# A planned attention and two-layer kernel: the planner counts its loads as one line, and memory features come from the transposed queries

## Chip, cores and metric

One core of one Trainium2 chip. The metric is the device time of one execution in microseconds; lower is better. The kernel before takes 1077.71 us (median of 3 runs, 1077.41 to 1077.94).

## What is computed

Attention with a memory (4 batches, 8 heads, 576 rows, 64 columns a head), then two layers of width 512 to 2048 to 512 on the 2304 rows:

```python
scores = scale * np.matmul(q, k.transpose(0, 1, 3, 2)), causal
a = np.exp(scores - scores.max(-1, keepdims=True))
a /= a.sum(-1, keepdims=True) + 1e-09
local = np.matmul(a, v)
phi(x) = np.where(x > 0, x, np.exp(x) - 1.0) + 1.0
mem_out = einsum('bhsd,bhde->bhse', phi(q), M_prev) / (einsum('bhsd,bhd->bhs', phi(q), z_prev)[..., None] + 1e-6)
x = g * mem_out + (1 - g) * local                 # g = sigmoid(beta), one for each head
layer 1: h = x @ w_in;  x = max(0.01 h, h) @ w_out
layer 2: h = x @ w_in;  out = (h - tanh(h)) @ w_out
```

## The kernel before

The work is cut into 32 units, each of two heads of one batch. A unit of kind A has the first 256 query rows, one of kind B the other 320. Four units of a batch and kind fill an x tile of 256 rows (the last 64 rows of each batch go to a ninth tile, R). A unit loads `qk` (transposed queries and keys), `rq` (queries in rows), `zb` and `mb` (z and M of its two heads), and `v`. Its memory part: phi of `rq` (ScalarE twice, L500 and L503; VectorE's max, L506), z times phi summed for each row tile and head (L513, four or six multiply-and-sum pairs on VectorE), reciprocal and gate (L519, L523), division of phi (L530), transposes of phi on TensorE (L547), a copy out of PSUM (pT, by the helper's L399 or L401), and the product with the block-diagonal M (L670), which opens the accumulator `o`. Its score part: scores (L584, L589: arrays of 64 rows, two heads side by side), maxima with the mask (L610), exponentials with sums (L630), for each row tile of two heads the sum with epsilon and gate and its reciprocal (L637, L641), scaling (L647 to L651: ScalarE, VectorE or POOL). Last come transposes of the weights (L691, L703), their copies, and the values (L725: arrays of 64 columns), added into `o`.

Layer 1 takes an x tile, splits it into a high and a low part (`xs`, lines L399, L401, L412 of the helpers) and sweeps over eight pairs of weight columns: `up` matmuls (L851), leaky step (L930), high and low part, `dn` matmuls (L953). The first four tiles go through two pairs first (four sweeps of 48 up and 48 dn matmuls each), then through the rest. The weights are 64-bit numbers: each 128x512 piece is loaded, turned into float32 by five steps (L783 on ScalarE, L786 to L799 on VectorE), and split (L399 to L412). Layer 2 has its weights converted beside layer 1, stored, and loaded again. It is written out by hand after the plan (L1060 on) and its matmuls are L851 and L1120.

The order of everything up to layer 2 comes from `Schedule` (L86). Each piece of work has engines with a cost each, a priority, and buffers from rings of fixed size (`RINGS`, L33). `run` (L146) goes through time on its own costs: whenever an engine is free it takes the piece of best priority whose inputs are done and whose buffers are free. A load costs its issue on SyncE, and a fixed latency (2300 to 4000 ns) later its readers may start, however many loads are under way. Attention has the better priority, layer matmuls fill in. What stands in the program is only the order on each engine; on the chip each instruction waits in its engine's queue for what it needs.

Of the kernel before, what the change touches and what calls it, by code (L numbers as in the profile page):

```python
# [9 lines left out]
F32 = mybir.dt.float32  # L10
# [26 lines left out]
}  # L37

# [42 lines left out]
class Op:  # L81
    __slots__ = (
        "alts", "fn", "prio", "lat", "alloc", "deps", "users", "left", "tiles", "end", "engine", "idx", "port")


class Schedule:  # L86


    def __init__(self, rings):
        self.rings = {k: [None] * n for k, n in rings.items()}  # L90
        self.count = {k: 0 for k in rings}
        self.made = {k: 0 for k in rings}
        self.ops = []

# [50 lines left out]

    def run(self):  # L146
        engines = ("pe", "act", "dve", "pool", "sp")
        free = {e: 1000.0 for e in engines}
# [11 lines left out]
        cold = 0.0  # L160
        port_free = 0.0
        events = [1000.0]
        t = -1.0
        while todo:
# [6 lines left out]
            while again:  # L171
                again = False
                for e in engines:
                    if free[e] > t:
                        continue
                    for i, (_, _, at, o) in enumerate(ready[e]):
# [25 lines left out]
                    free[e] = mine  # L202
                    heapq.heappush(events, mine)
# [24 lines left out]
CW = 256  # L228

# [15 lines left out]
def kernel(  # L245
# [40 lines left out]

    identr = const.tile([128, 128], F32R, name="identr")
    mask = const.tile([128, 512], BF16, name="mask")
    mask4 = const.tile([128, S // 2], BF16, name="mask4")
    omg4 = const.tile([128, H // 2], F32, name="omg4")  # L290
    mbs = [const.tile([128, 128], F32, name=f"mb{i}") for i in range(RINGS["mb"])]
    gate = const.tile([128, H], F32, name="gate")
# [22 lines left out]
    for m in mbs:  # L315
        nc.gpsimd.memset(m, 0.0)
# [3 lines left out]
    nc.sync.dma_start(out=gate, in_=beta.partition_broadcast(128))  # L320
    nc.scalar.activation(out=gate, in_=gate, func=AF.Exp, scale=-1.0)
    nc.vector.tensor_scalar(out=gate, in0=gate, scalar1=1.0, scalar2=None, op0=ALU.add)
    nc.vector.reciprocal(out=gate, in_=gate)
    nc.vector.tensor_scalar(out=omg, in0=gate, scalar1=-1.0, scalar2=1.0, op0=ALU.mult, op1=ALU.add)

    nc.vector.tensor_scalar(out=omg, in0=omg, scalar1=1e-30, scalar2=None, op0=ALU.max)
    nc.vector.reciprocal(out=omg, in_=omg)
    for i in range(2):
        p = slice(64 * i, 64 * i + 64)
        nc.vector.tensor_copy(out=omg4[p], in_=omg[p].rearrange("p (h j) -> p h j", j=2)[:, :, i])  # L330

# [48 lines left out]
    att = pa.enter_context(tc.tile_pool(name="att", bufs=1, side="right"))  # L380
    s_p = pa.enter_context(tc.tile_pool(name="s", bufs=3, space=PSUM, side="right"))
# [3 lines left out]
    x_h = {}  # L385
# [31 lines left out]
    class Unit:  # L417
# [14 lines left out]
        def declare(self, pr, prev):  # L432
# [15 lines left out]
            qk, rq, zb, mb, v_ = new("qk"), new("rq"), new("zb"), new("mb"), new("v" if kind == "B" else "va")  # L448
# [9 lines left out]
            def load_q(e):  # L458
                rq.tile = att.tile([128, 3, 2, 64], F32, name="rq", bufs=RINGS["rq"])
                for i, h in enumerate(heads):  # L460
                    nc.sync.dma_start(
                        out=rq.tile[:, 0:nq, i, :],
                        in_=q[b, h, q0 * 128:(q0 + nq) * 128, :].rearrange("(t p) d -> p t d", p=128))

            def load_mz(e):
                zb.tile = att.tile([128, 2, 64], F32, name="zb", bufs=RINGS["zb"])
                nc.sync.dma_start(
                    out=zb.tile.rearrange("p h d -> p (h d)"),
                    in_=z_prev[b, 2 * hp:2 * hp + 2, :].rearrange("h d -> (h d)").partition_broadcast(128))
# [15 lines left out]

            op([("sp", 600)], load_qk, alloc=[qk], lat=3000)
            op([("sp", 1000)], load_q, alloc=[rq], lat=2300)
            op([("sp", 1500)], load_mz, alloc=[zb, mb], lat=2300)
            op([("sp", 1000)], load_v, alloc=[v_], lat=2300)
# [3 lines left out]
            ph, dn = new("ph"), new("dnm")  # L493

            def flat(t):
                return t.rearrange("p t h d -> p (t h d)")[:, 0:nf]

            def phi_neg(e):
                ph.tile = att.tile([128, 3, 2, 64], F32, name="ph", bufs=RINGS["ph"])
                nc.scalar.activation(out=flat(ph.tile), in_=flat(rq.tile), func=AF.Relu, scale=-1.0)  # L500

            def phi_exp(e):
                nc.scalar.activation(out=flat(ph.tile), in_=flat(ph.tile), func=AF.Exp, scale=-1.0)  # L503

            def phi_max(e):
                nc.vector.scalar_tensor_tensor(  # L506
                    out=flat(ph.tile), in0=flat(rq.tile), scalar=1.0, in1=flat(ph.tile), op0=ALU.add, op1=ALU.max)

            def phi_den(e):
                dn.tile = att.tile([128, 3, 2], F32, name="dn", bufs=RINGS["dnm"])  # L510
                for i in range(nq):
                    for j in range(2):
                        nc.vector.tensor_tensor_reduce(  # L513
                            out=rq.tile[:, i, j, :], in0=ph.tile[:, i, j, :], in1=zb.tile[:, j, :], scale=1.0,
                            scalar=1e-6, op0=ALU.mult, op1=ALU.add, accum_out=dn.tile[:, i, j:j + 1])

            def den_inv(e):
                d = dn.tile[:, 0:nq, :]
                nc.vector.reciprocal(out=d, in_=d)  # L519

            def den_gate(e):
                d = dn.tile[:, 0:nq, :]
                nc.vector.tensor_tensor(  # L523
                    out=d, in0=d, in1=gate[:, 2 * hp:2 * hp + 2].unsqueeze(1).to_broadcast([128, nq, 2]),
                    op=ALU.mult)

            def phi_div(e):
                p = ph.tile[:, 0:nq].rearrange("p t h d -> p (t h) d")
                d = dn.tile[:, 0:nq].rearrange("p t h -> p (t h)")
                (nc.vector if e == "dve" else nc.gpsimd).tensor_tensor(  # L530
                    out=p, in0=p, in1=d.unsqueeze(2).to_broadcast([128, 2 * nq, 64]), op=ALU.mult)
# [9 lines left out]
            s, pT = new("s"), new("pT")  # L541

            def tr_p(e, s=s):
                pT.tile = att.tile([128, 320], F32, name="pT", bufs=RINGS["pT"])
                s.tile = s_p.tile([128, 512], F32, name="s")
                for i in range(nq):
                    nc.tensor.transpose(  # L547
                        s.tile[:, i * 128:(i + 1) * 128], ph.tile[:, i].rearrange("p h d -> p (h d)"), ident)

            def p_out(e, s=s):  # L550
                copy(e, pT.tile[:, 0:nqc], s.tile[:, 0:nqc])
# [670 lines left out]
```

## Time and profile before

| | |
|---|---|
| runs | 1077.41, 1077.71, 1077.94 us |
| profiled execution | span 1076.9 us from first to last instruction; no other time of it is given |
| TensorE matmul busy | 1042.5 us, 97% |
| VectorE, ScalarE, POOL busy | 754.0, 637.7, 100.3 us |
| mean granted clock of TensorE | 0.989 |
| DMA | 102.5 MB, 116403 packets |

A busy TensorE is not an engine at its peak, since matmuls are pipelined; the distance between starts tells what one costs. Two instructions of VectorE may overlap a little in the rows, so there too the distance between starts is the cost in a full queue.

### The profile page before, as it was taken

The page shows a single profiled execution, that of the slowest core. Times are in us where ns is not written, and L with a number is a line of the kernel's source. Part 1 is how long each engine was busy: PE and PEld are TensorE (multiplying, and loading weights), DVE is VectorE, ACT ScalarE, POOL GpSimd, SP SyncE. Part 2 cuts the span into 40 slices and gives each one's busy share as a digit, 9 for nine tenths or more (in the row PEclk, how much of TensorE's full clock was granted, in tenths as well). Part 3 has the DMA queues.
Part 4 walks back from the last instruction along what each step waited for, and adds up shares of the span by engine and source line. Part 5 has one row for each costly group of instructions (what it writes and reads, how often), then busy time and mean ns, then how long its engine had stood idle before and what let it go on. Part 6 is the DMA issues. An engine that isn't in the chain of part 4 may idle for free.

```text
span 1076.9 us, 20416 instructions
## 1 busy us (share of the span) xinstructions
PE 1042.5 (97%) x7488; PEld 918.8 (85%) x7488; DVE 754.0 (70%) x2049; ACT 637.7 (59%) x1357; POOL 100.3 (9%) x102
## 2 busy tenths in 40 slices
PE   4799999999999999999999999999999999999997
PEld 2477799778689978979999999999999999999996
DVE  6999999888677587664212366867777676777765
ACT  5889876777673277361101134766666666666664
POOL 0001000000000000000000000221222222222221
PEclk9699999999999999999999999999999999999999
DMA  7867763655644354243100055010101101010000
GB/s 223 250 177 222 225 203 107 159 153 153 183 141 137 119 165 147 89 132 102 40 2 21 10 158 186 1 41 1 40 2 39 40 1 40 1 40 20 1 20 20
DMA packets 116403, 102.52 MB, mean 95 GB/s; under 512 B 63824, under 2 KB 92496, under 8 KB 116304
## 3 DMA queue, kind: packets, MB, share of 16 engines
q1 hardware_dynamic: 115088, 99.91, 31.2%
q10 hardware_dynamic: 1216, 1.31, 0.4%
q8 instruction: 59, 0.97, 0.4%
q14 instruction: 40, 0.33, 0.1%
HBM read 78.65 MB, written 22.54 MB: 94 GB/s over the span
## 4 chain that ended last, share of the span: by engine, by line
PE 83%; DMA 6%; DVE 5%; ACT 4%; issue 1%; SPq 1%; DVEq 0%; ACTq 0%
PE up L851 36%; PE dn L1120 18%; PE dn L953 18%; PE s L703 3%; PE o L725 3%; PE s L584 3%; PE s L589 1%; PE o L670 1%; DMA cv<-in_moe_w_in_dram 1%; DMA qk<-in_qkt_dram 1%; ACT e L630 1%; DMA x2s<-g 1%; DMA w<-in_moe_w_in_dram 1%; DMA vs<-cv 1%; ACT e L647 1%
## 5 line engine op out<-in xcount | busy, mean ns | idle before, releaser
L851 PE MATMUL up<-xs,w 128*128 128x256 f32 x3456 | 454.6, 284 | 0.4 <-ACT g L930 0.4
L851 PEld LDWEIGHTS up<-xs,w 128*128 128x128 f32 x3456 | 434.1, 190 | 12.4 <-issue 5.6
L953 PE MATMUL dn<-gh,w 128*128 128x256 f32 x1152 | 160.1, 286 | 0.0
L953 PEld LDWEIGHTS dn<-gh,w 128*128 128x128 f32 x1152 | 146.0, 192 | 7.2 <-issue 6.5
L1097 DVE SCALAR_TENSOR_TENSOR gf<-u,w 128x512 f32<-128x512 f32 x72 | 85.8, 1192 | 83.4 <-ACT w L1094 83.4
L1120 PE MATMUL dn<-w,gh 128*128 128x512 f32 x568 | 143.2, 394 | 0.6 <-ACT gh L1107 0.6
L412 POOL TENSOR_TENSOR gl<-gf,gh 128x512 fp32r<-128x512 f32 x71 | 92.2, 1299 | 506.9 <-ACT gh L1107 503.3
L930 ACT ACTIVATE g<-up 128x512 f32<-128x512 f32 x72 | 42.9, 595 | 146.4 <-PE up L851 138.9
L1120 PEld LDWEIGHTS dn<-w,gh 128*128 128x128 f32 x568 | 101.6, 188 | 19.8 <-ACT gh L1107 0.8
L1089 ACT ACTIVATE u<-up 128x512 f32<-128x512 f32 x72 | 43.0, 598 | 123.7 <-PE up L851 123.7
L630 ACT ACTIVATE e<-e,mx 128x128 f32<-128x128 f32 (+4 forms) x144 | 82.7, 576 | 11.0 <-DVE mx L610 4.6
L953 PE MATMUL dn<-gl,w 128*128 128x256 f32 x576 | 84.5, 285 | 0.0
L401 DVE CAST gh<-g 128x512 fp32r<-128x512 f32 x35 | 14.9, 427 | 96.9 <-ACT g L930 96.8
L953 PEld LDWEIGHTS dn<-gl,w 128*128 128x128 f32 x576 | 75.2, 192 | 2.1 <-issue 1.9
L1120 PE MATMUL dn<-w,gl 128*128 128x512 f32 x284 | 76.2, 390 | 0.0
L610 DVE CUSTOM_DVE_ANT_0 e<-s,mask 128x128 f32<-128x128 f32 (+4 forms) x144 | 63.7, 483 | 10.6 <-PE s L584 6.6
L399 ACT ACTIVATE pt<-s 128x320 f32<-128x320 f32 (+4 forms) x149 | 58.2, 435 | 17.6 <-PE s L691 9.0
L584 PE MATMUL s<-qk 64*128 64x128 f32 (+3 forms) x256 | 53.8, 497 | 14.8 <-DMA qk<-in_qkt_dram 10.4
L703 PE MATMUL s<-identr,e 128*128 128x128 f32 x448 | 64.0, 287 | 3.9 <-ACT pT L399 2.8
L1120 PEld LDWEIGHTS dn<-w,gl 128*128 128x128 f32 x284 | 53.3, 188 | 11.9
L703 PEld LDWEIGHTS s<-identr,e 128*128 128x128 f32 x448 | 51.0, 145 | 12.9 <-ACT pT L399 3.4
L1091 DVE SCALAR_TENSOR_TENSOR hu<-up,u 128x512 f32<-128x512 f32 x72 | 49.7, 690 | 16.6 <-ACT u L1089 16.5
(105 smaller groups left out, 1334.2 us busy)
## 6 DMA issues: line engine op xcount, KB each, us to landing
w<-in_moe_w_out_dram SPq DMA_DIRECT2D x16, 512.0 KB, 5.1
cv<-in_moe_w_in_dram SPq DMA_DIRECT2D x32, 256.0 KB, 2.9
vs<-cv SPq DMA_DIRECT2D x64, 128.0 KB, 1.8
cv<-in_moe_w_out_dram SPq DMA_DIRECT2D x32, 256.0 KB, 2.9
v<-vs SPq DMA_DIRECT2D x32, 256.0 KB, 3.1
w<-in_moe_w_in_dram SPq DMA_DIRECT2D x14, 512.0 KB, 5.0
qk<-in_qkt_dram SPq DMA_DIRECT2D x16, 448.0 KB, 3.7
v<-in_v_dram SPq DMA_DIRECT2D x16, 320.0 KB, 3.5
```

What stands on the lines that cost most here:

```text
L399: nc.scalar.activation(out=out, in_=in_, func=AF.Copy)
L412: (nc.vector if e == "dve" else nc.gpsimd).tensor_tensor(out=out, in0=in_, in1=high, op=ALU.subtract)
L584: nc.tensor.matmul(ss[j].tile[:, c0:c0 + nn], lhsT=qk.tile[p, a:a + 128], rhs=qk.tile[p, kc:kc + nn], start=True, stop=True)
L610: nc.vector.tensor_tensor_reduce(out=out, in0=in0, in1=in1, scale=-scale, scalar=mx.tile[:, 0:1] if t == 4 and j else BIG, op0=ALU.add, op ...
L630: nc.scalar.activation(out=x, in_=x, func=AF.Exp, scale=-1.0, bias=mx.tile[:, k:k + 1], accum_out=sm.tile[:, j:j + 1])
L703: nc.tensor.transpose(ss[j].tile[:, a:a + 128], x, ident)
L851: nc.tensor.matmul(ps()[:, s, :], lhsT=w[:, wh * 512 + kt * 128:wh * 512 + (kt + 1) * 128], rhs=xs()[:, xh, kt, :], start=(kt == 0 and j = ...
L953: nc.tensor.matmul(dn[m // 2].tile[:, m % 2, :], lhsT=w[:, wh * 512 + m * 128:wh * 512 + (m + 1) * 128], rhs=gg.tile[:, s * 256:(s + 1) * ...
L1089: nc.scalar.activation(out=u, in_=h, func=AF.Square)
L1091: nc.vector.scalar_tensor_tensor(out=hu, in0=h, scalar=c4, in1=u, op0=ALU.mult, op1=ALU.mult)
L1097: nc.vector.scalar_tensor_tensor(out=g, in0=u, scalar=lin, in1=w, op0=ALU.mult, op1=ALU.add)
L1120: nc.tensor.matmul(dn[t], lhsT=g[:, c0:c0 + 128], rhs=w[:, wh * 512:(wh + 1) * 512], start=(p == 0 and s == 0 and j == 0), stop=(p == NP - ...
```

## The change

The memory part is turned round. phi is taken from the transposed queries in `qk`, so no `rq` is loaded and no phi transposed. M and z of all eight heads of a batch are loaded at once (`mz`: four pairs, 128 x 130, block-diagonal M with z as an extra column for each head; zeroed once by POOL) for four units. One product for each row tile gives result and denominator together in a score bank (128x130). VectorE adds epsilon and multiplies by 1/g, takes the reciprocal, and multiplies the result into `mo`; TensorE transposes `mo` straight into the accumulator `o`. The sums of the exponentials stand in one tile of five columns a unit: A has one epsilon step and one reciprocal for both row tiles, B two (sm, `GROUPS`), before all scalings.

The planner gets: a line of eight load lanes with sizes (`send`), so that a load lands after those ahead of it; no weight load (`calm`) while the line is over 6 us behind; a price for changing between TensorE's array shapes (`SWITCH`); other start times and costs. The two early weight loads are the first thing on ScalarE, and the gate's steps are part of the plan.

```diff
-    "qk": 2, "rq": 2, "xr": 1, "zb": 2, "mb": 2, ..., "pT": 1, "mx": 6, "sm": 6,
+    "qk": 2, "xr": 1, "mz": 2, ..., "mo": 1, "mx": 6, "sm": 3,
+LANES = 8
+SWITCH = {(0, 1): 88.0, (2, 1): 88.0, (0, 2): 45.0}
+CALM = 6000.0
+GROUPS = {"A": ((0, 2),), "B": ((0, 1), (1, 2), (2, 3))}
...
+    def send(self, t, sizes):
+        for size in sizes:
+            k = self.sent % LANES
+            t = max(t, self.lanes[k])
+            took = size / 375.0
+            self.landed = self.lanes[k] = max(self.landed + max(180.0, took), t + 2000.0 + took)
+            self.sent += 1
+            t += 600.0
+        return t
...
-        free = {e: 1000.0 for e in engines}
+        free = {"pe": 2500.0, "act": 2200.0, "dve": 3200.0, "pool": 4000.0, "sp": 800.0}
...
+                        if o.dma:
+                            if o.calm and self.landed > t + CALM:
+                                continue
+                            mine = self.send(t, o.dma)
+                            o.lat = self.landed - mine
                         if e == "pe":
+                            if o.mode != mode:
+                                mine += SWITCH.get((mode, o.mode), 0.0)
...
+    early_raw = [wts.tile([128, 1024], I32, name=f"w0_{f}") for f in range(EARLY)]
+    for f, raw in enumerate(early_raw):
+        nc.scalar.dma_start(out=raw..., in_=w1_in[...])
...
+    mzs = [att.tile([128, H // 2, 130], F32, name=f"mz{i}") for i in range(RINGS["mz"])]
+    for m in mzs:
+        nc.gpsimd.memset(m, 0.0)
...
             def load_mz(e):
+                mz.tile = mzs[mz.seq % RINGS["mz"]]
+                for j in range(2):
+                    rows, c = slice(j * 64, (j + 1) * 64), j * 65
+                    nc.sync.dma_start(out=mz.tile[rows, :, c:c + 64], in_=m_prev[b]...[j])
+                    nc.sync.dma_start(out=mz.tile[rows, :, c + 64], in_=z_prev[b]...[j])
...
-            op([("act", ACT(nf))], phi_neg, reads=[rq], alloc=[ph])
-            op([("act", ACT(nf))], phi_exp, reads=[ph], writes=[ph])
-            op([("dve", DVE(nf))], phi_max, reads=[rq, ph], writes=[ph])
-            op([("dve", 2 * nq * 145)], phi_den, reads=[ph, zb], writes=[rq], alloc=[dn])
-            op([("dve", 110)], den_inv, reads=[dn], writes=[dn], port=False)
-            op([("dve", 75)], den_gate, reads=[dn], writes=[dn])
-            op(lows(nf), phi_div, reads=[ph, dn], writes=[ph])
-            order["p"] = op([("pe", nq * 109 + 50)], tr_p, reads=[ph], alloc=[s, pT], after=in_order("p"))
-            free_op(copies(nqc, True), p_out, reads=[s], writes=[pT], port=False)
+            op([("act", ACT(nqc))], phi_neg, reads=[qk], alloc=[ph])
+            op([("act", ACT(nqc))], phi_exp, reads=[ph], writes=[ph])
+            op([("dve", DVE(nqc))], phi_max, reads=[qk, ph], writes=[ph])
+            order["p"] = op([("pe", nq * 195)], mem, reads=[ph, mz], alloc=[s, mo], after=in_order("p"))
+            free_op([("dve", 75)], den_gate, reads=[s, gates], alloc=[dn], port=False)
+            free_op([("dve", 110)], den_inv, reads=[dn], writes=[dn], port=False)
+            free_op([("dve", DVE(nf))], mem_out, reads=[s, dn], writes=[mo], port=False)
...
-            op([("pe", nqc * 1.67)], mem, reads=[mb, pT], alloc=[o])
+            op([("pe", nq * 109 - 60)], mem_tr, mode=2, reads=[mo], alloc=[o])
```

New lines that the order below names: product L535, its gate, reciprocal and multiplication L544, L551 and L554, transposes of the result L695, phi L520 to L527, scores L597, weight transposes L729, values L751, up L878, sums' steps L659 and L664, scaling L679, conversion L809 to L825, high and low parts L424, L426 and L437.

ScalarE, its first instructions, before (`gate` is the gate of beta, `w_0` the first early weight load):

```order
L321 ACT_TABLE_LOAD
L321 ACTIVATE gate<-gate 128x8
L342 DMA w_0_182<-in_moe_w_in_dram 128x4x256
L342 DMA w_1_186<-in_moe_w_in_dram 128x4x256
L500 ACTIVATE ph<-rq 128x256
L503 ACTIVATE ph<-ph 128x256
```

and now:

```order
L318 DMA w_0_65<-in_moe_w_in_dram 128x4x256
L318 DMA w_1_66<-in_moe_w_in_dram 128x4x256
L520 ACT_TABLE_LOAD
L520 ACTIVATE ph<-qk 128x256
L524 ACTIVATE ph<-ph 128x256
L809 ACTIVATE cv<-w_0_65 128x512
```

The loads stand ahead of the table load and of the gate, which comes later.

VectorE around the low halves of the first x tile (`xs`), before; four multiply-and-sum pairs (L513) stand just ahead of this piece:

```order
L641 RECIPROCAL sm<-sm 128x2
L637 SCALAR_TENSOR_TENSOR sm<-sm,omg 128x2
L519 RECIPROCAL dn<-dn 128x4
L412 TENSOR_TENSOR xs<-x,xs 128x512
L523 TENSOR_TENSOR dn<-dn,gate 128x4
L649 TENSOR_SCALAR e_650<-e_650,sm 128x128
L401 CAST xs<-x 128x512
L530 TENSOR_TENSOR ph<-ph,dn 128x256
L412 TENSOR_TENSOR xs<-x,xs 128x512
```

and now:

```order
L437 TENSOR_TENSOR xs<-x,xs 128x512
L664 RECIPROCAL sm<-sm 128x4
L815 TENSOR_SCALAR cv<-cv 128x512
L679 TENSOR_SCALAR e_497<-e_497,sm 128x128 x2
L679 TENSOR_SCALAR e_501<-e_501,sm 128x256 x2
L437 TENSOR_TENSOR xs<-x,xs 128x512
```

The second low half stood at row 209 of VectorE's order and stands at row 131; one reciprocal serves both row tiles, and all four scalings of a unit are VectorE's here.

TensorE around the first up matmul of layer 1 (`w_0` the first weights, `mb` and `mz` the memory's matrices), before:

```order
L584 MATMUL s<-qk 128x128 x2
L584 MATMUL s<-qk 128x256 x2
L547 MATMUL s<-identr,ph 128x128 x2
L851 MATMUL up<-xs,w_0_276 128x256 x6
L670 MATMUL o<-pT,mb_69 128x256
L725 MATMUL o<-pt,va 64x256 x2
```

and now:

```order
L729 MATMUL s<-identr,e_497 128x128
L729 MATMUL s<-identr,e_501 128x128 x2
L878 MATMUL up<-xs,w_0_258 128x256 x9
L535 MATMUL s<-mz_168,ph 128x130 x2
L878 MATMUL up<-xs,w_0_258 128x256 x3
L878 MATMUL up<-xs,w_1_311 128x256 x12
L695 MATMUL o<-identr,mo 128x128 x2
L751 MATMUL o<-pt,va 64x256 x2
```

The product into a score bank comes first, layer matmuls stand between it and the transposes into `o`.

## Rows read from the trace of the kernel before

**Rows 1.** Busy time by stretch: us, engines' busy us (x count), clock, DMA share, GB/s

```profile
10.00:56.00 46.00, 32.28 (x143) 19.40 (x144) 42.11 (x200) 37.64 (x115) 0.00 (x0) 0.78 0.82 250
56.00:106.00 50.00, 48.20 (x380) 38.51 (x380) 49.58 (x257) 46.50 (x146) 3.66 (x5) 1.00 0.72 198
200.00:400.00 200.00, 196.21 (x1497) 161.24 (x1497) 146.76 (x563) 120.77 (x295) 1.53 (x10) 1.00 0.53 152
540.00:660.00 120.00, 120.00 (x1002) 120.00 (x1002) 47.48 (x85) 25.45 (x43) 0.00 (x0) 1.00 0.21 66
```

The engines stand in the order PE (TensorE matmul), PEld (its weight loads), DVE (VectorE), ACT (ScalarE), POOL.

**Rows 2.** The same view, two stretches of 5 us

```profile
25.00:30.00 5.00, 1.03 (x5) 0.28 (x2) 3.73 (x17) 4.50 (x16) 0.00 (x0) 0.64 1.10 300
55.00:60.00 5.00, 4.29 (x34) 3.06 (x31) 5.00 (x22) 3.46 (x13) 0.00 (x0) 1.00 0.92 225
```

**Rows 3.** Order of time, first 12 us: start, us, engine, line, what [idle before]

```profile
0.80 1.28 ACT L321 ACT_TABLE_LOAD   x1 [0.80 <-PEq L1207]
...
3.73 1.00 ACTq L342 DMA_DIRECT2D w<-in_moe_w_in_dram  x2
...
5.60 0.55 SPq L454 DMA_DIRECT2D qk<-in_qkt_dram  x1
...
9.33 0.66 ACT L783 ACTIVATE cv<-w 128x512 f32<-128x512 f32 x1 [3.48 <-DMA w<-in_moe_w_in_dram]
10.02 0.43 DVE L786 TENSOR_SCALAR cv<-cv 128x512 f32<-128x512 f32 x1 [3.71 <-ACT cv L783]
```

**Rows 4.** Order of time, VectorE alone, 41.6 to 44.8 us

```profile
41.49 0.28 DVE L649 TENSOR_SCALAR e<-e,sm 128x128 f32<-128x128 f32 x1
41.69 0.16 DVE L637 SCALAR_TENSOR_TENSOR sm<-sm,omg 128x2 f32<-128x2 f32 x1
41.76 0.29 DVE L610 CUSTOM_DVE_ANT_0 e<-s,mask 128x128 f32<-128x128 f32 x1
...
42.18 0.42 DVE L610 CUSTOM_DVE_ANT_0 e<-s,mask 128x256 f32<-128x256 f32 x1
...
42.95 0.41 DVE L506 SCALAR_TENSOR_TENSOR ph<-rq,ph 128x256 f32<-128x256 f32 x1
43.27 0.35 DVE L649 TENSOR_SCALAR e<-e,sm 128x256 f32<-128x256 f32 x1
43.53 0.22 DVE L513 CUSTOM_DVE_ANT_0 rq<-ph,zb 128x64 f32<-128x64 f32 x1
...
44.11 0.69 DVE L412 TENSOR_TENSOR w<-cv,w 128x512 fp32r<-128x512 f32 x1
44.71 0.17 DVE L519 RECIPROCAL dn<-dn 128x4 f32<-128x4 f32 x1
```

**Rows 5.** Order of time, TensorE alone, 76 to 106 us

```profile
76.58 0.60 PE L670 MATMUL o<-pT,mb 128*128 128x256 f32 x2
77.10 0.87 PE L725 MATMUL o<-pt,va 128*64 128x256 f32 x8
77.90 0.50 PE L953 MATMUL dn<-gl,w 128*128 128x256 f32 x2
78.24 0.82 PE L703 MATMUL s<-identr,e 128*128 128x128 f32 x6
78.81 1.43 PE L953 MATMUL dn<-gh,w 128*128 128x256 f32 x10
80.17 0.93 PE L584 MATMUL s<-qk 64*128 64x128 f32 x8
81.03 0.74 PE L953 MATMUL dn<-gh,w 128*128 128x256 f32 x4
...
105.95 1.24 PE L851 MATMUL up<-xs,w 128*128 128x256 f32 x9
```

A unit's values, scores and product stand as eight, eight and two matmuls in the trace.

**Rows 6.** The same view, 41 to 43 us

```profile
41.67 1.55 PE L725 MATMUL o<-pt,va 128*64 128x256 f32 x8
```

**Rows 7.** Waits of TensorE: who for whom, us in total, times, longest

```profile
PE s L703 <- ACT pT L399: 2.8, 1, 2.8
```

More of the change, by code (lines that the diff above doesn't have):

```diff
@@ L82 @@
     __slots__ = (
-        "alts", "fn", "prio", "lat", "alloc", "deps", "users", "left", "tiles", "end", "engine", "idx", "port")
+        "alts", "fn", "prio", "lat", "alloc", "deps", "users", "left", "tiles", "end", "engine", "idx", "port", "dma", "calm", "mode")
 class Schedule:
@@ L159, in run @@
         todo = len(self.ops)
-        cold = 0.0
+        cold, mode = 0.0, 0
         port_free = 0.0
-        events = [1000.0]
+        events = sorted(set(free.values()))
         t = -1.0
@@ L289 @@
     mask4 = const.tile([128, S // 2], BF16, name="mask4")
-    omg4 = const.tile([128, H // 2], F32, name="omg4")
-    mbs = [const.tile([128, 128], F32, name=f"mb{i}") for i in range(RINGS["mb"])]
-    gate = const.tile([128, H], F32, name="gate")
+    omg5 = const.tile([128, H // 2, 5], F32, name="omg5")
+    ginv = const.tile([128, H], F32, name="ginv")
     omg = const.tile([128, H], F32, name="omg")
@@ L319 @@
     nc.vector.memset(thr_t, -T2)
[L320 to L330, printed above, removed]
     wt = [[None] * NF for m in range(2)]
@@ L502, in phi_exp @@
             def phi_exp(e):
-                nc.scalar.activation(out=flat(ph.tile), in_=flat(ph.tile), func=AF.Exp, scale=-1.0)
+                nc.scalar.activation(out=ph.tile[:, 0:nqc], in_=ph.tile[:, 0:nqc], func=AF.Exp, scale=-1.0)
             def phi_max(e):
                 nc.vector.scalar_tensor_tensor(
[L507 to L531, printed above, removed]
@@ new lines, in den_gate, with den_inv @@
+            def den_gate(e):
+                dn.tile = att.tile([128, 3, 2], F32, name="dn", bufs=RINGS["dnm"])
+                nc.vector.scalar_tensor_tensor(
+                    out=dn.tile[:, 0:nq], in0=banked()[:, :, :, 64], scalar=1e-6,
+                    in1=ginv[:, 2 * hp:2 * hp + 2].unsqueeze(1).to_broadcast([128, nq, 2]),
+                    op0=ALU.add, op1=ALU.mult)
+            def den_inv(e):
+                d = dn.tile[:, 0:nq]
+                nc.vector.reciprocal(out=d, in_=d)
@@ L559, in declare @@
             made = {}
+            sm = new("sm")
+            sums = 2 * nq - (kind == "B")
+            first, expos, inv = [], {}, {}
             for tiles in ([[0, 1]] if kind == "A" else [[2], [3], [4]]):
@@ L727, in pv @@
                             rhs=pt.tile[:, at + j * w:at + (j + 1) * w], start=False, stop=kt == nk - 1)
[L729 removed]
+            op([("pe", 801 if kind == "A" else 2205)], pv, mode=1, reads=[v_, o] + list({id(x): x for x in pts.values()}.values()),
                writes=[o])
@@ L803, in convert @@
         if early:
-            sc.op([("act", 500)], load, alloc=[raw], lat=3600, prio=(-2, 0))
-        else:
-            op([("sp", 500)], load, alloc=[raw], lat=2600, after=after)
-        first = op([("act", ACT(n))], c_abs, reads=[raw], alloc=[g])
+            raw.tile = early_raw[f]
+            sc.op([("sp", 1)], lambda e: None, alloc=[raw], lat=3500.0 + 1400.0 * f, prio=(-2, 0))
+        else:
+            op([("sp", 500)], load, alloc=[raw], dma=[1024 * n], calm=True, after=after)
+        first = op([("act", ACT(n) + 45)], c_abs, reads=[raw], alloc=[g])
         op([("dve", DVE(n / 2))], c_max, reads=[g], writes=[g])
@@ L986, in layer1, with load_beta, gate_exp, gate_rest @@
                 sop(copies(512, True), x2_out, reads=[dn[i]], alloc=[x2], port=False)
-            sop([("sp", 500)], x2_store, reads=[x2], writes=[x2_h[n] if p1 == NP else xp_h[n][i]], lat=2300)
+            sop([("sp", 500)], x2_store, reads=[x2], writes=[x2_h[n] if p1 == NP else xp_h[n][i]], dma=[262144])
+    def load_beta(e):
+        nc.sync.dma_start(out=ginv, in_=beta.partition_broadcast(128))
+    def gate_exp(e):
+        nc.scalar.activation(out=ginv, in_=ginv, func=AF.Exp, scale=-1.0)
+    def gate_rest(e):
+        nc.vector.tensor_scalar(out=ginv, in0=ginv, scalar1=1.0, scalar2=None, op0=ALU.add)
+        nc.vector.reciprocal(out=omg, in_=ginv)
+        nc.vector.tensor_scalar(out=omg, in0=omg, scalar1=-1.0, scalar2=1.0, op0=ALU.mult, op1=ALU.add)
+        nc.vector.tensor_scalar(out=omg, in0=omg, scalar1=1e-30, scalar2=None, op0=ALU.max)
+        nc.vector.reciprocal(out=omg, in_=omg)
+        pairs = omg.rearrange("p (h j) -> p h j", j=2)
+        for i in range(2):
+            nc.vector.tensor_copy(out=omg5[:, :, 2 * i:2 * i + 2], in_=pairs)
+        for i in range(2):
+            p = slice(64 * i, 64 * i + 64)
+            nc.vector.tensor_copy(out=omg5[p, :, 4], in_=pairs[p, :, i])
+    gates = sc.new(None)
+    sc.op([("sp", 600)], load_beta, writes=[gates], prio=(0, 0.1), dma=[4096])
+    sc.op([("act", 210)], gate_exp, reads=[gates], writes=[gates], prio=(0, 0.1))
+    sc.op([("dve", 1600)], gate_rest, reads=[gates], writes=[gates], prio=(0, 0.1))
     prev = None
```

159 lines of the change are left out of this document (87 added, 72 removed), and 2 rows, old and new, of the table RINGS.

## The prediction

> **What bounds the kernel now.** I read the profile in this order. First the busy times by stretch [rows 1]: from 540 to 660 us TensorE is busy all the time, 1002 matmuls in 120 us, so a 128x256 layer matmul takes 0.12 us; from 200 to 400 it is busy 196.2 of 200. There only less work on TensorE itself, or those 3.8 us, can give time. Before 106 us it is otherwise: from 10 to 56 TensorE is busy 32.3 of 46, VectorE 42.1, ScalarE 37.6; from 56 to 106 VectorE is busy 49.6 of 50. So I then read VectorE's order of time [rows 4]: one instruction starts as the last ends, and the steps between starts are the prices used below. Last I read the first 10 us [rows 3]: VectorE's stream of attention and weight conversion begins at 10.02, after a wait of 3.71 for the ScalarE step at 9.33, which waited for the first weight load, issued by ScalarE only at 3.73, behind the gate.
>
> How much of the span is lost ahead of the full stretch can be counted at one point, where the first up matmul of the third x tile starts: 105.95 [rows 5]. Ahead of it TensorE's order holds 172 layer matmuls (20.6 us at 0.12), 16 units of scores (13.6 at 0.85, 80.17 to 81.03), 12 of values (9.6 at 0.80, 77.10 to 77.90), 108 transposes (11.8 at 0.109: 78.24 to 78.81 for six, and about 0.08 that the next row pays), 12 memory products (5.2 at 0.43) and 25 changes into the half-array shape of scores and values (2.2 at 0.09: ten layer matmuls from 78.81 to 80.17 take 1.36, of which 1.20 are theirs and 0.07 the transposes'). Sum 63.0. **Lost by then: 43 us.** The limit is VectorE: 90.6 us of its steps stand between its first conversion (10.02) and the second half of that x tile, done in 95.9 us, a factor of 1.059.
>
> **The change, part by part.**
> *VectorE up to the third x tile*, by its two orders and the steps of [rows 4]. Denominators by multiply-and-sum: 52 pairs at 0.146 (four from 43.53 to 44.11), 7.6 us, now none. Small instructions: 84 at 0.08 (6.9) become 50, plus nine of the gate that used to stand before 10 us (4.8). Maxima: 30 of 128 and 30 of 256 columns (0.21, 0.345: 16.7) become 28 and 26 (14.9), since fewer units are taken ahead. Copies out of PSUM 8, now 6, at 0.335 (2.7 to 2.0). Scaling moves onto VectorE: 12 at 0.20 and 9 at 0.26 (4.7) become 16 and 18 (7.9). The max of phi and the division or new product: 24 at 0.335 in both (8.0). Weights, x tiles and layer results: 44.0 and 44.9 (0.60 for 512 columns, half of it in the fast form). Sums 90.6 and **82.5**. The new product reads PSUM where the division read SBUF; the maxima read PSUM too, at 0.345 for 256 columns, so I give it the same price.
>
> *The start.* The two early loads are now ScalarE's first instructions. They can go out when its first instruction started before, 0.80, in place of 3.73 [rows 3], so the stream starts 2.9 us earlier, at 7.1. On SyncE's queue the two q loads, z and M of a unit go and one load for eight heads comes, in four pieces, each priced like the issue of a qk load, 0.55 [rows 3]. It must wait for POOL's zeroing of buffers four times as large as before; queued behind it are v, beta and the second qk load, which I expect 1 to 1.5 us later than 5.60. Unit 1's maxima stand behind some 4 us of VectorE work after 7.1, so this is covered; uncovered it costs 1.5.
>
> With the same factor the third x tile is ready at 7.1 + 82.5 x 1.059 = 94.5. TensorE's order holds less ahead of it now: 182 layer matmuls (21.8), 14 units of scores (11.9), 12 of values (9.6), 96 transposes (10.5), 26 pieces of memory product (5.7), 13 shape changes (1.2), sum 60.7. Lost: 33.8. **Gain 43.0 - 33.8 = 9.2 us.** Bounds: with no idle VectorE 7.1 + 82.5 = 89.6, a gain of 14.1; with weights landing no earlier and the idle share of 10 to 56 us (46 / 42.1 = 1.09) 100, a gain of 3.6. I take the measured factor, being that of the same mix of work. ScalarE follows: it loses the copies of transposed phi and scaling, about as large a part as VectorE.
>
> *TensorE, whole program.* 80 transposes of phi go, 80 of the result come: nothing. The product: 32 of 256 or 320 columns (16 x 0.43 + 16 x 0.54 by columns = 15.6) become 80 of 130 columns, by the same 1.69 ns a column 0.22 each, 17.6: +2.0 (if the first columns hide under weight loads, 0). Changes into the half-array shape, counted in the orders, 80 before and 68 after: -1.1. Together +0.9.
>
> *Loads as one line, and calm.* The plan no longer starts work on a load that it wrongly thinks landed. Of waits there are 3.8 us between 200 and 400 us [rows 1]: 0 to -4, I take -1.
>
> *The clock, a page against the trace.* From 55 to 60 us the granted clock was 1.00, that is 2.4 GHz, at the first layer matmuls [rows 2]; from 25 to 30, with TensorE busy 1.0 of 5 us, it was 0.64, part of that time at 1.2 GHz. At the low clock eight value matmuls took 1.55 us [rows 6] against 0.87 [rows 5]. So I add nothing for it. The Trainium skill, TensorE: Matmul & The Clock Gate, section HAM oscillation, says that waits between bursts of matmuls throttle the engine again and again, each burst then starting at half rate. By that rule a denser VectorE with the layers beginning some 12 us earlier, among units that still wait, could see them start at 1.2 GHz; the sum would be some 9 us worse.
>
> Sum: -9.2 + 0.9 - 1.0 = -9.3. The profiled execution's span is 1076.9, 0.8 below the median of the runs, 1077.7; what lies around the span is not touched. **1068.4 us.**
>
> **The rivals.**
> *Slower: the product's bank.* Transposed phi left PSUM in one copy. Now three VectorE steps must follow each other (add and gate, reciprocal, product) before one of the three score banks is free, and TensorE's queue stands still if its next row wants that bank. The three take 0.08 + 0.08 + 0.34 by step, 0.7 to 0.9 with each one's own end, so 26 us over 32 units if nothing covers them: 1068 + 26 = 1094. It decides from 0.3 us a unit on. For it: one wait for the copy of phi cost 2.8 us before [rows 7]. Against: in the new order layer matmuls follow 25 of the 32 products.
> *Loads set the pace.* From 10 to 56 us the DMA engines were 0.82 busy [rows 1]. Conversion keeps its place in the queue while units go faster, so weights may land late and VectorE stand before them as it did at 10 us. Then the low bound of the start holds: 1077.7 - 3.6 + 0.9 = 1075. That the plan's new costs do nothing is the same case.
> *Half clock at the first layers.* The third tile comes earlier, but the first sweep, 11.5 us of layer matmuls, runs at 1.2 GHz; by the two value rows (1.55 / 0.87) that is 9 us more, and the gain is gone: 1077.5. Against it stands the clock of 1.00 at 55 to 60 us [rows 2]. The rule of the Trainium skill above would give this.
> *More than forecast.* VectorE without idle time (-14.1) and the waits of 200 to 400 us half gone (-2), with the product at its low price (-1.1): 1077.7 - 17.2 = 1060.5; all 4 us gone: 1058.
>
> **How the numbers follow.** Forecast 0.60; more 0.14; loads 0.10; half clock 0.05; slower by the bank 0.11. The forecast's own range is 1064 to 1073. To hold 8 in 10 the whole range reaches from 1057 (the fullest gain, a us beyond) to 1076 (the low bound with the product's full price of 2.0). A measurement can tell about 0.2%, 2.2 us: faster is below 1075.5. The forecast, the larger gain and most of the loads case lie there: 0.82. Within 0.2%: the clock case and the rest of the loads, 0.07. Slower: 0.11.
>
> **What would show it.** Right: VectorE's first conversion near 7 us; the first up matmul of the third x tile at 93 to 97; VectorE busy over 0.9 up to there; multiply-and-sum pairs gone; TensorE's busy time from 540 to 660 unchanged. Wrong: TensorE waiting on the new dn or mo steps by over 5 us in all (bank); VectorE or ScalarE idle ahead of conversion for over 5 us (loads); a granted clock of 0.5 after the first up matmul (clock); a third tile before 90.

## The result, and the profile after

The changed kernel takes 1064.88 us (median of 4 runs, 1063.26 to 1066.34) against 1077.56 (the three runs above and a fourth, 1074.99): a ratio of 0.9882 (95% interval 0.986 to 0.9903), 12.7 us faster. The forecast was 1068.4. The profiled execution has a span of 1064.6 us at a granted clock of 0.992.

Busy times of the changed kernel by stretch, as [rows 1], and, in the last two rows, the start of its layer matmuls:

```profile
10.00:56.00 46.00, 34.23 (x209) 25.95 (x209) 41.20 (x158) 35.30 (x103) 1.87 (x3) 0.85 0.83 242
56.00:106.00 50.00, 47.50 (x410) 40.25 (x406) 49.74 (x193) 43.39 (x130) 2.58 (x4) 1.00 0.61 181
200.00:400.00 200.00, 194.46 (x1513) 163.30 (x1514) 139.32 (x447) 113.83 (x278) 2.00 (x10) 0.99 0.48 141
540.00:660.00 120.00, 120.00 (x1003) 120.00 (x1002) 49.89 (x88) 28.18 (x48) 0.00 (x0) 1.00 0.23 71
43.80:46.80 3.00, 3.00 (x15) 2.86 (x14) 3.00 (x8) 1.48 (x3) 0.00 (x0) 0.50 0.35 124
46.80:49.30 2.50, 2.50 (x17) 2.50 (x17) 2.50 (x10) 2.19 (x6) 0.00 (x0) 0.71 0.90 300
```

Before 106 us more matmuls are done (209 and 410 against 143 and 380); VectorE is as full as before. Between 200 and 400 us TensorE idles 5.5 us, not 3.8. From 540 to 660 nothing has changed. The first layer matmuls, from 43.8 on, ran at a granted clock of 0.50 (1.2 GHz), then 0.71.

Order of time of the changed kernel, as [rows 3], [rows 5] and [rows 7]: the start, the third x tile, the new product, and TensorE's longest waits of the whole program:

```profile
0.81 1.03 ACTq L318 DMA_DIRECT2D w<-in_moe_w_in_dram  x2
...
3.89 0.42 ACT L520 ACTIVATE ph<-qk 128x256 f32<-128x256 f32 x1 [0.74 <-DMA qk<-in_qkt_dram]
...
6.10 0.43 DVE L812 TENSOR_SCALAR cv<-cv 128x512 f32<-128x512 f32 x1 [0.89 <-ACT cv L809]
...
7.35 0.43 SPq L479 DMA_DIRECT2D qk<-in_qkt_dram  x1
```

```profile
43.81 2.27 PE L878 MATMUL up<-xs,w 128*128 128x256 f32 x9
45.93 1.23 PE L535 MATMUL s<-mz,ph 128*128 128x130 f32 x4
...
49.33 0.38 PE L695 MATMUL o<-identr,mo 128*128 128x128 f32 x2
...
51.29 0.71 PE L535 MATMUL s<-mz,ph 128*128 128x130 f32 x4
51.76 1.68 PE L878 MATMUL up<-xs,w 128*128 128x256 f32 x12
...
95.97 0.52 PE L878 MATMUL up<-xs,w 128*128 128x256 f32 x3
```

```profile
PE s L597 <- DMA qk<-in_qkt_dram: 4.6, 2, 3.9
PE o L695 <- DVE mo L554: 4.0, 2, 3.1
PE s L535 <- DMA mz<-in_z_prev_dram: 3.0, 1, 3.0
```

The conversion begins at 6.10 (10.02 before), the third tile at 95.97 (105.95). A product of two pieces costs 0.47 us by its start distance at full clock (51.29 to 51.76; a product stands as four matmuls in the trace).

Two things are not as forecast. The lead of 10.0 us at the third tile is 5.0 at the end of layer 1: the first `dn` matmul of layer 2 starts at 667.49, before at 672.50. And layer 2, whose code and order the change doesn't touch, takes 397.1 us from there to the end, before 404.4. Order of time of TensorE in layer 2, before (L851) and after (L878), each followed by the busy times of one stretch there:

```profile
810.88 3.04 PE L851 MATMUL up<-xs,w 128*128 128x256 f32 x24
813.77 2.02 PE L1120 MATMUL dn<-w,gh 128*128 128x512 f32 x8
```

```profile
700.00:1040.00 340.00, 340.00 (x2171) 309.23 (x2170) 245.09 (x309) 227.71 (x384) 77.83 (x60) 1.00 0.07 23
```

```profile
808.99 2.96 PE L878 MATMUL up<-xs,w 128*128 128x256 f32 x24
811.79 2.00 PE L1172 MATMUL dn<-w,gh 128*128 128x512 f32 x8
```

```profile
700.00:1040.00 340.00, 340.00 (x2209) 309.80 (x2208) 248.59 (x315) 231.71 (x390) 79.28 (x61) 1.00 0.07 23
```

24 up matmuls take 2.89 us before and 2.80 after: 120.4 and 116.7 ns each (means of all steps from 700 to 1040 us: 120.3, scattered from 115 to 133, and 116.8). The engine is "busy" all the time in both at the same clock; only the count shows it.

### The profile page after: what moved, and what is told of

It reads as the page before. It is cut to its first block, busy times and chain, and to the rows that moved or that the text cites. A ratio compares the mean times of both kernels' runs of the same rounds, so it can differ in the third digit from the quotient of the medians.

```text
span 1064.6 us, 20001 instructions
## 1 busy us (share of the span) xinstructions
PE 1030.4 (97%) x7584; PEld 921.5 (87%) x7584; DVE 731.5 (69%) x1707; ACT 619.7 (58%) x1309; POOL 105.4 (10%) x111
## 4 chain that ended last, share of the span: by engine, by line
PE 87%; DMA 6%; ACT 3%; DVE 2%; issue 1%; SPq 0%; ACTq 0%; DVEq 0%
PE up L878 35%; PE dn L1172 18%; PE dn L980 17%; PE s L729 5%; PE o L751 4%; PE s L597 4%; DMA cv<-in_moe_w_in_dram 2%; PE s L535 2%; PE s L602 1%; DMA vs<-cv 1%; DMA qk<-in_qkt_dram 1%; PE o L695 1%; DMA w<-in_moe_w_out_dram 1%; DMA w<-in_moe_w_in_dram 1%; ACT e L643 1%
## 5 line engine op out<-in xcount | busy, mean ns | idle before, releaser
L878 PE MATMUL up<-xs,w 128*128 128x256 f32 x3456 | 447.4, 283 | 0.6 <-ACT g L957 0.6
L878 PEld LDWEIGHTS up<-xs,w 128*128 128x128 f32 x3456 | 429.0, 190 | 11.2 <-issue 5.0
L437 POOL TENSOR_TENSOR gl<-gf,gh 128x512 fp32r<-128x512 f32 x71 | 92.4, 1302 | 498.7 <-ACT gh L1159 498.7
L426 DVE CAST gh<-g 128x512 fp32r<-128x512 f32 x36 | 15.3, 426 | 96.3 <-ACT g L957 96.3
L729 PE MATMUL s<-identr,e 128*128 128x128 f32 x448 | 65.5, 286 | 7.9 <-DVE e L679 2.9
L424 ACT ACTIVATE pt<-s 128x320 f32<-128x320 f32 (+4 forms) x147 | 57.2, 435 | 18.7 <-PE s L729 10.9
L729 PEld LDWEIGHTS s<-identr,e 128*128 128x128 f32 x448 | 53.2, 147 | 12.2 <-issue 4.0
L597 PE MATMUL s<-qk 64*128 64x128 f32 (+3 forms) x256 | 50.9, 497 | 8.8 <-DMA qk<-in_qkt_dram 4.6
L1152 DVE COPY_PREDICATED gf<-mk,up 128x512 f32<-128x512 int32 x72 | 53.6, 745 | 7.8 <-DVE up L1151 0.5
```

What stands on the lines that cost most here:

```text
L424: nc.scalar.activation(out=out, in_=in_, func=AF.Copy)
L437: (nc.vector if e == "dve" else nc.gpsimd).tensor_tensor(out=out, in0=in_, in1=high, op=ALU.subtract)
L597: nc.tensor.matmul(ss[j].tile[:, c0:c0 + nn], lhsT=qk.tile[p, a:a + 128], rhs=qk.tile[p, kc:kc + nn], start=True, stop=True)
L729: nc.tensor.transpose(ss[j].tile[:, a:a + 128], x, ident)
L878: nc.tensor.matmul(ps()[:, s, :], lhsT=w[:, wh * 512 + kt * 128:wh * 512 + (kt + 1) * 128], rhs=xs()[:, xh, kt, :], start=(kt == 0 and j = ...
L1152: nc.vector.copy_predicated(out=g, mask=mk.bitcast(I32), data=h)
```

## Experiments

Medians of before stood at 1077.2 to 1078.7 us beside these runs; each ratio is to the runs of before on the same chip, with its 95% interval.

### Where layer 2 got faster: addresses

The change moves two `mb` buffers out of the constants and alters small ones, 960 B a partition in all; weights and everything after them on the left side of SBUF move down by that, while the split x tiles of layer 2 (right side) stay. "Distance" is from the weights' address to that of `xs` (in layer 1 also of `gh` and `gl`), modulo 512 B; it is worked out from the kernels' tiles, the traces hold no addresses.

**e1_addr**, on the kernel before:

```diff
-    mbs = [const.tile([128, 128], F32, ...)]
+    pad = const.tile([128, 16], F32, name="pad")
...
+    mbs = [att.tile([128, 128], F32, ...)]
```

> The kernel before, with its M buffers moved from the constants into the attention pool and a pad of 64 B a partition in their place, so that all later tiles on the left side of SBUF (weights, x tiles, layer-2 scratch) stand 960 B lower, as in the changed kernel; the order of the work is the same. Theory (addresses set the pace of layer 2): the mean step of up matmuls from 700 us on falls from 120.3 to about 116.8 ns as in the changed kernel, layer 2 takes 397 us in place of 404, the whole about 1070.5 us (1069.5 to 1072). Rival (layer 2 differs from run to run, or by what precedes it): steps and time stay, 1077.5 (1076.5 to 1078.5).

1070.47 us, ratio 0.9941 (0.9928 to 0.9953). Its layer 2:

```profile
700.00:1040.00 340.00, 340.00 (x2205) 309.70 (x2204) 248.13 (x313) 232.79 (x393) 79.87 (x62) 1.00 0.07 23
```

The distance of layer 2 is 96 in the kernel before, 32 here and in the changed kernel. 2205 matmuls in place of 2171, step 116.8 ns, layer 2 in 397.6 us. **6.9 of the 12.7 us come from addresses alone**; the rest of the change is worth 5.6 (1070.5 to 1064.9; by the intervals each is known to 1 or 2 us).

**e2_pad32**, on the changed kernel:

```diff
+    pad_p = p1.enter_context(tc.tile_pool(name="pad", bufs=1))
+    pad = pad_p.tile([128, 8], F32, name="pad")
     x_p = p1.enter_context(tc.tile_pool(name="x", bufs=2))
```

> The changed kernel with 32 B a partition put between the weights and the layer-1 tiles, so that the distance from the weights to the x tiles of layer 1 is 32 B more (a multiple of 512 B as it stands); layer 2 keeps its addresses. Theory (the distance of the two operands sets the pace): the step of 120.0 ns between 540 and 660 us falls to about 117, layer 1 ends up to 11 us earlier, 1054 to 1060 us. Rival (120 ns is the price of a layer-1 matmul): 120.0 ns and 1063 to 1067.

1057.36 us, 0.9815 (0.9801 to 0.9828). Layer 1, the changed kernel's stretch first, then this one's:

```profile
540.00:640.00 100.00, 100.00 (x836) 100.00 (x835) 35.58 (x64) 20.03 (x34) 0.00 (x0) 1.00 0.15 48
```

```profile
540.00:640.00 100.00, 100.00 (x860) 100.00 (x859) 39.89 (x71) 22.39 (x38) 0.00 (x0) 1.00 0.20 64
```

24 more matmuls in the same 100 us: 116.7 ns. So 0.12 us, which the prediction took as the price of a layer matmul, was the price at distance 0. (The change moves the weights and the layer-1 tiles together by 960 B; their distance stays 0, and so did the 120.0 ns.)

**e5_pad64** has 64 B there (`[128, 16]`), and a 96 B tile ahead of layer 2's `xs`:

> The changed kernel with 64 B between the weights and the layer-1 tiles, and 96 B ahead of the split x tiles of layer 2, so that in both layers the x tiles stand 64 B (of 128) away from the weights. So far: distance 0 gave 120.0 ns a step, 32 gave 116.7, 96 gave 120.3 with scatter. Theory a (only a part of the distances is fast, and 64 is as fast as 32 or faster): layer 1 at 116.7 or below and layer 2 at 116.8 or below, 1056 to 1059. Theory b (64 is as slow as 0): 120.0 in both layers, layer 2 takes 7 us more than in the changed kernel: 1070 to 1073.

1059.49 us, 0.9828 (0.9815 to 0.9841). Its two stretches:

```profile
540.00:640.00 100.00, 100.00 (x852) 100.00 (x850) 39.82 (x71) 21.91 (x37) 0.00 (x0) 1.00 0.19 60
700.00:1040.00 340.00, 340.00 (x2205) 311.20 (x2205) 248.10 (x314) 232.62 (x392) 79.03 (x61) 1.00 0.07 23
```

Both layers' up step is 117.8 ns, between the two theories but near the first; e12_best below shows that 32 B can give it too. In layer 2 the `dn` step fell at the same time (226.7 ns, 228.9 in the changed kernel), so the stretch holds as many matmuls.

### The start: the early loads

**e3_early**, the kernel before with the change's early loads alone:

```diff
+    for f, raw in enumerate(early_raw):
+        nc.scalar.dma_start(out=raw..., in_=w1_in[...])
...
-            sc.op([("act", 500)], load, alloc=[raw], lat=3600, prio=(-2, 0))
+            sc.op([("act", 500)], lambda e: None, alloc=[raw], lat=3600, prio=(-2, 0))
```

> The kernel before with one thing of the change alone: the two early weight loads are the first instructions of ScalarE's queue, the plan's order is the same. Theory (the start is bound by VectorE's stream, which begins with these weights): the first conversion starts 3 to 4 us earlier, near 6 to 7 us, the third x tile's first up matmul near 102 to 103 in place of 105.95, and the whole is 2 to 4 us faster, 1074 to 1075.5. Rival (qk or other loads hold the stream just as long, or later waits give it back): within 1 us, 1077 to 1078.

1077.31 us, 0.9997 (0.9988 to 1.0006): nothing. Order of time of its start:

```profile
0.81 1.03 ACTq L289 DMA_DIRECT2D w<-in_moe_w_in_dram  x2
...
1.72 0.95 SPq L467 DMA_DIRECT2D rq<-in_q_dram  x2
...
9.10 0.42 ACT L506 ACTIVATE ph<-rq 128x256 f32<-128x256 f32 x1 [4.96 <-DMA rq<-in_q_dram]
...
9.87 1.21 ACT L789 ACTIVATE cv<-w 128x512 f32<-128x512 f32 x2
...
10.55 0.43 DVE L792 TENSOR_SCALAR cv<-cv 128x512 f32<-128x512 f32 x1
```

And of the kernel before:

```profile
1.72 0.95 SPq L461 DMA_DIRECT2D rq<-in_q_dram  x2
...
4.98 0.42 ACT L500 ACTIVATE ph<-rq 128x256 f32<-128x256 f32 x1 [1.05 <-DMA rq<-in_q_dram]
```

The weights are issued at 0.81, but ScalarE's phi, ahead of the conversion in its queue, now waits for `rq` until 9.10; in the kernel before it had `rq` at 4.98. `rq` is issued at 1.72 in both. With the weights' 1 MB ahead of it, it lands 4.1 us later (the DMA share was 0.96 to 1.09 from 4 to 7 us). So the wait only moved from the weights to `rq`. The changed kernel has no `rq`: its phi starts at 3.89, on a `qk` issued at 0.80.

**e11_gatefirst**, the changed kernel with the gate ahead again (a 128 B tile, so all left addresses move 128 B):

```diff
+    first = const.tile([128, 32], F32, name="first")[:, 0:H]
+    nc.sync.dma_start(out=first, in_=beta.partition_broadcast(128))
+    nc.scalar.activation(out=first, in_=first, func=AF.Exp, scale=-1.0)
     early_raw = [...]
```

> The changed kernel, with a load of beta and an exponential of it put ahead of the two early weight loads on ScalarE's queue, as the kernel before had it, in tiles that nothing reads; all else in the same order. Theory (the loads' place is worth the 2.9 us of the prediction): issue near 3.7 us in place of 0.8, first conversion near 9 us, third x tile and whole 2 to 3 us later: 1067 to 1068. Rival (they are worth nothing, as they were alone on the kernel before): 1064 to 1066.

1068.03 us, 0.9909 (0.9894 to 0.9924), 3.2 over the changed kernel, as the theory said, but for another reason in the main. Its start in order of time, and its layer 2:

```profile
8.67 0.43 DVE L815 TENSOR_SCALAR cv<-cv 128x512 f32<-128x512 f32 x1 [2.73 <-ACT cv L812]
```

```profile
700.00:1040.00 340.00, 340.00 (x2195) 311.10 (x2195) 246.68 (x313) 231.20 (x389) 79.39 (x61) 1.00 0.07 23
```

The conversion starts 2.6 us later. The third tile at 95.90 is no later than in the changed kernel's profile (95.97), but 2.9 us later than in that of e7_nocalm below (93.00), which has the same order and, from 10 to 56 us, the same clock of 0.93; profiles of one order differ by as much. Layer 2 takes 399.4 us, 2.3 more: its up step is 118.9 ns at a distance of 416 B, 32 modulo 128 like the 32 B that give 116.8. About 0.9 us is left for the loads' place, which isn't clear of noise.

### The planner

**e7_nocalm** takes out the two lines of `calm`.

> The changed kernel with the line of loads, but without calm. Theory (calm costs, since weight loads are held back and ScalarE's and TensorE's queues then stand behind them at 170 to 370 us): 1060 to 1062, and the waits of TensorE between 200 and 400 us fall from 5.5 to about 2 us. Rival (the line itself costs, calm is nothing): 1064 to 1066, waits as in the changed kernel.

1064.70 us, 0.9873 (0.9858 to 0.9888). The order on every engine is the changed kernel's, row for row: the line is never 6 us behind where a weight load is due. It is thus the same program twice, and shows the scatter of one profile: its third tile starts at 93.00, 3 us earlier, its clock from 10 to 56 us was 0.93, not 0.85.

**e4_flat**, on the changed kernel:

```diff
-                            if o.calm and self.landed > t + CALM:
-                                continue
-                            mine = self.send(t, o.dma)
-                            o.lat = self.landed - mine
+                            o.lat = 3000.0 if max(o.dma) > 300000 else 2300.0
```

> The changed kernel, but its planner takes for every load a fixed latency, 2.3 us or 3.0 for a weight piece, with neither line nor calm, as before. My theory (the line is worth about 1 us, the new memory path and the start carry the gain): 1063 to 1068. Rival (the line carries most of the gain in the attention stretch): 1070 to 1075, with more waits of TensorE between 100 and 500 us than the changed kernel has.

1060.36 us, 0.9851 (0.9834 to 0.9868), below both theories: against these latencies the line as written costs 4.5 us by the medians (the two intervals just meet). The 3.0 us holds for loads of over 300000 B alone; a weight piece, 262144 B, gets 2.3. **e6_oldcost** is this with `SWITCH = {}` and `free = {e: 1000.0 for e in engines}`:

> The changed kernel with its planner costs as before: fixed load latencies, no calm, no price for changing array shapes, every engine free at 1 us. What is left of the change is the memory part from the transposed queries, the grouped sums and the early loads. Theory (these carry the gain, the planner's new costs are worth nothing or less): 1059 to 1064, like the kernel with fixed latencies alone. Rival (the price of shapes or the start times carry the gain): 1068 to 1075, with more shape changes or a later third x tile.

1066.59 us, 0.99 (0.9882 to 0.9917), between the theories. With `SWITCH = {}` alone the order is the same row for row, so the start times do nothing and the price of shapes is worth about 6.2 us (1066.6 to 1060.4), though the changes into the half-array shape are 68 without it and 69 with it: it reorders, it doesn't save changes. The memory part, the grouped sums, the early loads and the plan's other altered costs are left with 3.9 (1070.5 to 1066.6). Sums are grouped in kind A alone: by `GROUPS`, B has an epsilon step and a reciprocal for each of its three row tiles, not two.

Why does the line cost? Its weight pieces land, in the plan, 2.7 us after their issue begins (0.6 and 2.1, the median over its loads); fixed latencies say 2.8, the plan before said 3.1; the chip takes 2.8 to 3.0 (DMA issues of the changed kernel's page). Waits of ScalarE between 106 and 420 us for weight pieces, in the kernel before, the changed one and e4_flat:

```profile
ACT cv L783 <- DMA cv<-in_moe_w_out_dram: 12.0, 8, 4.0
ACT cv L783 <- DMA cv<-in_moe_w_in_dram: 7.8, 7, 2.7
```

```profile
ACT cv L809 <- DMA cv<-in_moe_w_in_dram: 22.7, 13, 4.8
ACT cv L809 <- DMA cv<-in_moe_w_out_dram: 17.6, 7, 4.5
```

```profile
ACT cv L806 <- DMA cv<-in_moe_w_in_dram: 15.7, 10, 4.9
ACT cv L806 <- DMA cv<-in_moe_w_out_dram: 13.2, 7, 2.7
```

How such a wait can reach TensorE, in the changed kernel's order of time:

```profile
285.74 0.44 ACT L809 ACTIVATE cv<-cv 128x256 f32<-128x256 f32 x1 [1.62 <-DMA cv<-in_moe_w_out_dram]
...
288.70 0.47 ACT L520 ACTIVATE ph<-qk 128x320 f32<-128x320 f32 x1 [0.80 <-DMA qk<-in_qkt_dram]
...
289.58 0.76 ACT L677 ACTIVATE e<-e,sm 128x576 f32<-128x576 f32 x1
...
290.39 1.82 PE L729 MATMUL s<-identr,e 128*128 128x128 f32 x8 [1.88 <-ACT e L677]
```

A scaling that TensorE needs stands on ScalarE behind a conversion that waited 1.62 us for its weights and a phi that waited 0.80 for `qk`. **e9_line26** changes one number of the changed kernel, **e10_flat26** one of e4_flat:

```diff
-max(self.landed + max(180.0, took), t + 2000.0 + took)
+max(self.landed + max(180.0, took), t + 2600.0 + took)
```

```diff
-                            o.lat = 3000.0 if max(o.dma) > 300000 else 2300.0
+                            o.lat = 3000.0 if max(o.dma) > 300000 else 2600.0
```

> The changed kernel with one number altered: the line takes 2.6 us in place of 2.0 from issue to landing, beside the size. A weight piece then lands 3.3 us after its issue in the plan (3.1 before the change, 2.7 in the change, 2.8 with fixed latencies). ScalarE's waits for weight loads between 106 and 420 us were 19.8, 40.3 and 28.9 us in these three. Theory (the line's loss is that it thinks weights land too early): waits of 20 to 30 us and 1058 to 1062 us. Rival (holding loads in a line costs whatever the latency): waits near 40 us, 1063 to 1067.

> The kernel with fixed latencies, 2.6 in place of 2.3 us for all but the largest loads, the value that the kernel before had for weights. Same theory: ScalarE's waits for weight loads fall from 28.9 to 20 to 25 us, 1057 to 1060 us. Rival (the gain of fixed latencies was an accident of one order): 1062 to 1067.

e9_line26: 1060.00 us, 0.9835 (0.9819 to 0.9851), as the theory said. ScalarE's waits in the same stretch, and busy times between 200 and 400 us:

```profile
ACT cv L809 <- DMA cv<-in_moe_w_out_dram: 14.9, 6, 5.0
ACT cv L809 <- DMA cv<-in_moe_w_in_dram: 10.3, 5, 5.1
```

```profile
200.00:400.00 200.00, 197.29 (x1548) 165.42 (x1547) 143.87 (x459) 113.51 (x279) 1.37 (x9) 1.00 0.48 141
```

25.2 us of waits in place of 40.3, TensorE is busy 2.8 us more. But e10_flat26: 1065.50 us, 0.9886 (0.9867 to 0.9904), the rival's value, with waits of 31.6 us in place of 28.9. So the same 0.3 to 0.6 us in a latency gained 4.9 with the line and lost 5.1 without. Of the prices above each is thus that of one order; that later landings help in general isn't shown.

### Together

**e8_flatpad** is e4_flat with e2's 32 B, **e12_best** is e9_line26 with them.

> Fixed latencies and the 32 B together, on the changed kernel. If the two gains (4.5 and 7.5 us against the changed kernel's 1064.9) add up: 1052 to 1054. If the faster layer steps meet the same late weights: 1055 to 1058.

> The line at 2.6 us and the 32 B between weights and layer-1 tiles, together on the changed kernel. If they add up as measured apart (1064.9 - 4.9 - 7.5): 1052.5, 1051 to 1054. If the faster layer steps meet late weights, as with fixed latencies (1055.9, of which 1052.9 was expected): 1055 to 1057.

e8_flatpad: 1055.91 us, 0.9793 (0.978 to 0.9805), 3 us short of the sum; in its trace layer 2 takes 400.0 us in place of 397, with one wait of 3.1 for the first high part (`dn` for ScalarE's `gh`). e12_best: **1053.70 us**, 0.9775 (0.9757 to 0.9792), nearly the full sum, with no such wait; it is the fastest, 11 us below the changed kernel. Its layer-1 stretch, to be set beside those of e2_pad32 (860 matmuls) and e5_pad64 (852):

```profile
540.00:640.00 100.00, 100.00 (x851) 100.00 (x851) 43.41 (x77) 24.30 (x41) 0.00 (x0) 1.00 0.24 76
```

With the tiles at e2_pad32's addresses its step is 117.8 ns here, not 116.7. Both values occur within one run: e2_pad32 has 117.6 from 300 to 440 us and 116.7 from 460 on, e12_best 116.7 from 420 to 460. So of 0, 32 and 64 B in layer 1 only 0 stands apart; what chooses between 116.7 and 117.8 stays open.

## Why the prediction came out right, and where it didn't

The time lay 3.5 us below the forecast, in its range; but two errors cancelled in part. Forecast for the work was -9.3; shown are -5.6 by order and work and -6.9 by addresses. Without the addresses the kernel would have stood near 1072, still in the range; that it came out below the forecast is luck.

*The start* (-9.2). The conversion began at 6.10 (7.1 forecast), the third tile at 95.97 (94.5). With 60.7 us of work ahead of it 35.3 are lost, a gain of 7.7, and 10.7 in the second profile of the same order. At that point the size holds. The first 2.9 us of it, put down to the early loads alone, aren't theirs alone: by themselves they gave nothing, since `rq` then landed at 9.10 in place of 4.98, and taken back they left about 0.9 at the end. The prediction priced the load that is moved forward, not those that it passes.

*TensorE's pieces* (+0.9). A piece of the product took 0.23 us (0.22 forecast); the shape changes weren't measured again.

*The line and calm* (-1). This step failed: the waits that were to shrink grew. TensorE's idle time between 200 and 400 us went from 3.8 to 5.5, and the lead of 10.0 us at the third tile shrank to 5.0 at the end of layer 1; at 2.6 us in the line the idle time is 2.7. Calm never acts. Against fixed latencies of 2.3 us the line costs 4.5 us, against 2.6 it gains 0.6, so that even the sign of its price is that of one order. The prediction took a better model of loads for fewer waits without holding its 2.0 us against the trace.

*The clock* (0). Nine up matmuls from 43.81 took 2.12 us, twice 1.08, after a wait of 2.89. The Trainium skill, TensorE: Matmul & The Clock Gate, section HAM oscillation, has bursts after waits start at half rate, and here the trace agrees. That of e5_pad64 doesn't: in the same order, after a wait of 3.08 us at the same place, the granted clock was 1.00 (40.6 to 46.1 us).

```profile
40.66 1.31 PE L881 MATMUL up<-xs,w 128*128 128x256 f32 x9
43.13 0.71 PE L538 MATMUL s<-mz,ph 128*128 128x130 f32 x4 [1.16 <-DVE ph L530]
...
46.09 0.41 PE L698 MATMUL o<-identr,mo 128*128 128x128 f32 x2 [0.48 <-DVE mo L557]
```

From the first up matmul to the first transposes into `o` it took 5.43 us at full clock (40.66 to 46.09) and 5.52 in the changed kernel (43.81 to 49.33), since at full clock TensorE waits for VectorE instead. So the half clock cost next to nothing there, not the 9 us of that rival, and for this stretch the 0 held.

*What isn't touched.* "TensorE's busy time from 540 to 660 unchanged" held, and so 0.12 us was right for layer 1. That layer 2 keeps its time was never said but assumed: the sum was made of added, removed and moved work. It failed by 7 us.

*The rivals.* TensorE's waits on `mo` are 4.0 us, none after 106 us: the bank isn't the bound. Loads may set the pace in part after 106 us: ScalarE's waits for weights there are 40.3 us and were 19.8, but e10_flat26 shows that they don't settle the time by themselves. Two of the prediction's signs of being wrong thus showed, a granted clock of 0.5 at the first up matmuls and an engine idle ahead of conversion for over 5 us, and neither decided the time.

## What to carry to other kernels

When a change alters the size of any tile, compare the step of unchanged matmuls before and after, by the counts of a stretch: a pad of 32 B was worth more here (7.5 us) than the rewriting of the memory part with all that went with it (5.6). A load that is moved forward delays those that it passes: price them too, and look at who waits for them. And a planner's cost is tested by several values: orders that differ by one latency lay 5 us apart. One profile says little of one stage: the third tile of the same order started at 95.97 and at 93.00.

## What the runs showed of the hardware

A 128x256 float32-typed matmul with 128x128 weights, back to back at full clock, takes by the distance of its moving tile from its weights in SBUF (modulo 512 B): 120.0 ns at 0, 116.7 to 117.8 at 32 (both in e2_pad32 and in e12_best), 117.8 at 64 in layer 1; 116.8 at 32, 120.3 with scatter at 96, 118.9 at 416 and 117.8 at 448 in layer 2. In layer 1 32 and 64 B thus can't be told apart. Distance modulo 128 alone doesn't set the step (32 and 416 in layer 2), nor do the addresses alone (the two values at 32). The rule behind it stays open, as does why layer 2's 512-column matmuls moved from 228.9 to 226.7 ns when only the x tiles had been shifted.

A load was delayed by those issued ahead of it: the same two `rq` loads, issued at 1.72 us, were there by 4.98 us, and with two 512 KB weight loads ahead of them only by 9.10.
